# Keeping TensorE in its tiled modes between two tiled groups of matmuls: a bridge of 128x32 column tiles

## The chip, the cores and the metric

The kernel runs on one core of one Trainium2 chip. The metric is the device time of one execution in microseconds (us). Single executions of one kernel scatter by about 0.3%. "Same" means within 2%. PE is TensorE, PEld its weight loads, DVE VectorE, ACT ScalarE, POOL GpSimd, SP SyncE.

## The reference, cut to what matters

```python
def _A_ref(x, wqkv, wo):                       # linear attention, 32 heads of 16
    qkv = ...(x @ wqkv)...
    pq, pk = phi(q), phi(k)
    kv = jnp.einsum("bhsd,bhse->bhde", pk, v)
    z  = jnp.einsum("bhsd->bhd", pk)
    o  = (pq @ kv) / (pq . z)
    return o... @ wo
def _B_ref(x, w1, b1, w2, b2):                 # MLP across the 2048 tokens
    h = _layernorm(x)
    u = _gelu(jnp.einsum("bsd,sf->bdf", h, w1) + b1)      # F = 1792
    return (jnp.einsum("bdf,fs->bds", u, w2) + b2)^T
out = g * _A_ref(...) + (1 - g) * _B_ref(...)  # g = sigmoid(sum(x * gate_w))
```

x is 2048 x 512, all in bf16.

## The kernel before

The kernel never forms v. It computes G = x^T phi(k), then kv per head from wv and G, then W2 = kv Wo, so that attention ends as one matmul of normalised phi(q) with W2. kv and kv Wo need only the diagonal blocks of the heads, so both use PE as an array of small tiles. A mode is named by the rows and columns of one tile: 128x32 cuts the 128x128 array into four tiles side by side (column tiles), 32x32 into sixteen, and 128x128 is the array as a whole. A change of mode is a step from one cut to another. The stationary operand is the weights, which stay in the array; the columns of the other operand (512 in an MLP step) move through it.

```python
def kv_matmuls():                               # 64 matmuls, mode 128x32 (4 column tiles)
    kvps = bank("kvps")
    for j in range(ND):
        for k in range(ND):
            for q in range(0, P, Q32):
                c = slice(j * P + q, j * P + q + Q32)
                mm(kvps[q : q + Q32, j * Q32 : (j + 1) * Q32], wv_sb[:, k, c], gT[:, k, c],
                   k == 0, k == ND - 1, tile_position=(0, q))
    nc.vector.tensor_tensor(out=kvT..., in0=kvps..., in1=maskQ..., op=ALU.mult)   # kvT: what kv Wo reads

def w2_matmuls():                               # "kv Wo": 16 matmuls, mode 32x32 (16 tiles)
    w2ps.extend(bank("w2ps") for _ in range(ND))
    for j in range(ND):
        for i in range(NQ):
            r, c = i * Q32, (i ^ j) * Q32
            mm(w2ps[j][c : c + Q32, :], kvT[r : r + Q32, j, :], wo_sb[r : r + Q32, j, :],
               True, True, tile_position=(r, c))
```

Both stand among the blocks of the first MLP matmul. A block makes 128 rows of u from 16 steps (t) of 128x128x512 matmuls into one PSUM bank; a GELU on ACT empties it:

```python
for j in range(NB0, NF):                        # 11 blocks
    c, jj = divmod(j, FB)
    acc = bank("uacc")
    for t in range(NT):                         # 16 steps
        mm(acc[:], w1c[c][:, t, jj * P : (jj + 1) * P], hs[:, t, :], t == 0, t == NT - 1)
    gelu(j, acc)
    i = j - NB0
    if i == 2:
        kv_matmuls()
    elif i == 3:
        w2_matmuls()
    if 3 <= i < 3 + ND:
        w2_copies(i - 3)                        # ACT empties the banks of kv Wo
    ...                                         # normaliser of phi(q) on ACT and DVE, gate, loads
```

So PE goes 128x128, 128x32 (kv), 128x128 (16 steps), 32x32 (kv Wo), 128x128: four changes of mode.

## Time and profile before

| | before |
|---|---|
| time, median of 3 runs | 163.76 us (163.11 to 163.76) |
| span of the profiled run | 161.6 us |
| PE busy | 156.9 us, 97% |
| DVE, ACT busy | 124.8 us, 72.8 us |

The page of the kernel before, part 1 (busy time, share of the span, instructions) and part 4 (the chain of work that ended last, by engine and by line):

```profile
PE 156.9 (97%) x802; PEld 72.1 (45%) x817; DVE 124.8 (77%) x272; ACT 72.8 (45%) x112; POOL 7.3 (4%) x17
...
PE 97%; DVE 1%; issue 1%
...
PE uacc L110 30%; PE yps L110 30%; PE aps L110 9%; PE kacc L110 8%; PE qacc L110 8%; PE gacc L110 8%; PE wps L110 2%; PE pt L110 1%; DVE xT L208 0%; PE kvps L110 0%; PE w2ps L110 0%; DVE ot L494 0%; PE pt L331 0%
```

PE is the bound, and kv and kv Wo (kvps, w2ps) round to 0% of the chain. The page counts 802 matmuls beside 817 weight loads: 15 matmul records are missing from this trace. Where a record is missing, the view shows a hole of one step that was none.

The timeline of PE around kv and kv Wo, before (start, duration in us, line, operation, tile, shapes, count; neighbours of one kind are merged):

```profile
67.40 0.38 PE L110 MATMUL uacc<-hs,w1c 128*128 128x512 bf16 x1
67.70 0.66 PE L110 MATMUL kvps<-gT,wv_sb 128*32 128x32 bf16 x64
68.30 3.63 PE L110 MATMUL uacc<-hs,w1c 128*128 128x512 bf16 x15
71.86 0.43 PE L110 MATMUL w2ps<-wo_sb,kvT 32*32 32x512 bf16 x16
72.22 0.39 PE L110 MATMUL uacc<-hs,w1c 128*128 128x512 bf16 x1
```

PE looks busy without a break, because the record of a matmul (379 ns) is longer than the pitch at which matmuls follow one another (216 ns). The cost of a change of mode is to be read from starts, not from busy time. To the nanosecond, from the single records of the same trace:

```
from -> to, before                             starts (us)         apart   steady pitch
last MLP step -> first of kv (128x32)          67.396 -> 67.705    309 ns  216
last of kv -> first MLP step                   68.183 -> 68.299    116 ns  8
last MLP step -> first of kv Wo (32x32)        71.547 -> 71.856    309 ns  216
last of kv Wo -> first MLP step                71.906 -> 72.223    317 ns  about 216
that MLP step -> the next one                  72.223 -> 72.449    226 ns  216
```

From 10 us to the last matmul these are the only places in the kernel where two matmuls start further apart than 222 ns, missing records apart. Apart from its start-up, the kernel has no other hole on PE.

### The profile page before, as it was taken

What the parts mean: (1) busy time and instruction counts of PE and PEld (TensorE: products, weight loads), DVE (VectorE), ACT (ScalarE), POOL (GpSimd) and SP (SyncE); (2) the same over time, 40 slices, a digit from 0 to 9 for tenths busy, and PEclk for the clock granted to TensorE, in tenths of its full rate; (3) what the DMA queues carried; (4) which work ended last, traced back from release to release, by engine and by line L of the source; (5) the groups of instructions that cost most, each with busy time, mean ns of one, the idle gap of its engine ahead of it and who ended that gap; (6) DMA issues with size and microseconds to landing.
All of it is one profiled execution on the core that took longest, in us unless ns stands there. A gap on an engine that the chain in (4) does not pass through costs nothing.

```text
span 161.6 us, 2188 instructions
## 1 busy us (share of the span) xinstructions
PE 156.9 (97%) x802; PEld 72.1 (45%) x817; DVE 124.8 (77%) x272; ACT 72.8 (45%) x112; POOL 7.3 (4%) x17
## 2 busy tenths in 40 slices
PE   7999999999999999999999999999999999999993
PEld 3444444444444444444444444444444444444452
DVE  1799999957999999588599996669999999611112
ACT  3363386648667473324987123343333333111110
POOL 3000611200110000000000000000000000000000
PEclk9999999999999999999999999999999999999999
DMA  4999999999990006700940488601000001110001
GB/s 158 214 217 247 238 313 320 349 349 347 343 229 1 0 0 202 252 4 0 315 144 2 158 296 265 222 32 36 33 32 32 32 32 47 50 37 32 32 32 32
DMA packets 29241, 22.94 MB, mean 142 GB/s; under 512 B 7696, under 2 KB 29200, under 8 KB 29232
## 3 DMA queue, kind: packets, MB, share of 16 engines
q1 hardware_dynamic: 28256, 21.89, 45.6%
q10 hardware_dynamic: 864, 0.79, 1.5%
q0 software_dynamic: 112, 0.14, 0.8%
q8 instruction: 6, 0.10, 0.2%
q14 instruction: 3, 0.02, 0.1%
HBM read 19.01 MB, written 2.10 MB: 131 GB/s over the span
## 4 chain that ended last, share of the span: by engine, by line
PE 97%; DVE 1%; issue 1%
PE uacc L110 30%; PE yps L110 30%; PE aps L110 9%; PE kacc L110 8%; PE qacc L110 8%; PE gacc L110 8%; PE wps L110 2%; PE pt L110 1%; DVE xT L208 0%; PE kvps L110 0%; PE w2ps L110 0%; DVE ot L494 0%; PE pt L331 0%
## 5 line engine op out<-in xcount | busy, mean ns | idle before, releaser
L110 PE MATMUL uacc<-hs,w1c 128*128 128x512 bf16 x220 | 51.3, 379 | 0.2
L110 PE MATMUL yps<-uT,w2c 128*128 128x512 bf16 (+2 forms) x233 | 50.6, 366 | 0.3
L110 PEld LDWEIGHTS <-w2c 128*128 128x128 bf16 x238 | 22.8, 98 | 25.9
L110 PEld LDWEIGHTS <-w1c 128*128 128x128 bf16 x224 | 21.7, 98 | 26.1 <-issue 0.2
L481 ACT ACTIVATE a_sc<-aps,c,gg 128x512 f32<-128x512 f32 x16 | 12.4, 775 | 34.1 <-PE aps L110 30.5
L494 DVE SCALAR_TENSOR_TENSOR ot<-yps,c,a_sc 128x512 bf16<-128x512 f32 (+2 forms) x17 | 12.2, 716 | 16.1 <-PE yps L110 15.1
L325 ACT ACTIVATE uT<-uacc,bcol 128x512 bf16<-128x512 f32 x14 | 9.3, 686 | 18.2 <-PE uacc L110 18.1
L110 PE MATMUL kacc<-wk_sb,xT 128*128 128x512 bf16 x63 | 16.0, 380 | 0.3 <-DVE xT L208 0.2
L110 PE MATMUL qacc<-xT,wq_sb 128*128 128x512 bf16 x61 | 16.1, 379 | 0.2
L110 PE MATMUL aps<-W2sb,pqT 128*128 128x512 bf16 x63 | 16.2, 379 | 0.1
L110 PE MATMUL gacc<-pk,xs 128*128 128x512 bf16 x63 | 15.6, 379 | 0.0
L390 DVE STREAM_TRANSPOSE zT<-pz 128x512 f32<-128x512 f32 x16 | 11.3, 705 | 4.9 <-ACT pz L389 4.9
L212 ACT ACTIVATE e<-qacc 128x512 bf16<-128x512 f32 x16 | 9.6, 597 | 9.2 <-PE qacc L110 9.2
L389 ACT ACTIVATE pz<-pqT,zcol 128x512 f32<-128x512 bf16 x16 | 11.4, 714 | 4.8 <-DVE ot L494 4.7
L252 ACT ACTIVATE hs<-xs,nmr,rstd 128x512 bf16<-128x512 bf16 x16 | 12.8, 805 | 1.8 <-DVE nmr L246 1.8
L212 ACT ACTIVATE e<-kacc 128x512 bf16<-128x512 f32 x16 | 9.3, 594 | 9.2 <-PE kacc L110 9.1
L399 DVE STREAM_TRANSPOSE rex<-rd 128x512 bf16<-128x512 bf16 x16 | 11.4, 711 | 0.6
L216 DVE SCALAR_TENSOR_TENSOR pqT<-qacc,e 128x512 bf16<-128x512 f32 x16 | 11.1, 692 | 0.6
L216 DVE SCALAR_TENSOR_TENSOR pk<-kacc,e 128x512 bf16<-128x512 f32 x16 | 11.1, 692 | 0.6
L392 DVE TENSOR_REDUCE den<-zT 128x32 f32<-128x512 f32 x16 | 11.0, 686 | 0.6
L110 PEld LDWEIGHTS <-xs 128*128 128x128 bf16 x76 | 7.4, 104 | 8.5 <-DMA xs<-in_A_x_dram 1.0
L213 DVE TENSOR_SCALAR e<-e 128x512 bf16<-128x512 bf16 x32 | 9.0, 281 | 2.8 <-ACT e L212 2.8
(59 smaller groups left out, 101.0 us busy)
## 6 DMA issues: line engine op xcount, KB each, us to landing
w2c<-in_B_w_dram SPq DMA_DIRECT2D x8, 896.0 KB, 5.8
w1c<-in_B_w_dram SPq DMA_DIRECT2D x2, 2048.0 KB, 16.0
w1c<-in_B_w_dram SPq DMA_DIRECT2D x3, 1024.0 KB, 12.4
out_dram<-ot SPq DMA_DIRECT2D x13, 128.0 KB, 1.7
xs<-in_A_x_dram SPq DMA_DIRECT2D x3, 512.0 KB, 4.9
wq_sb<-in_A_wqkv_dram SPq DMA_DIRECT2D x1, 512.0 KB, 6.1
wv_sb<-in_A_wqkv_dram SPq DMA_DIRECT2D x1, 512.0 KB, 11.7
wo_sb<-in_A_wo_dram SPq DMA_DIRECT2D x1, 512.0 KB, 10.3
```

Source lines behind the costliest of these rows:

```text
L110: nc.tensor.matmul(o, lhsT=lhsT, rhs=rhs, start=start, stop=stop, **kw)
L212: nc.scalar.activation(out=e[:], in_=acc[:], func=ACT.Exp)
L213: nc.vector.tensor_scalar(out=e[:], in0=e[:], scalar1=1.0, scalar2=PHI_EPS, op0=ALU.min, op1=ALU.add)
L216: nc.vector.scalar_tensor_tensor(out=dst, in0=acc[:], scalar=0.0, in1=e[:], op0=ALU.max, op1=ALU.add)
L252: nc.scalar.activation(out=hs[:, t, :], in_=xs[:, t, :], func=ACT.Identity, scale=rstd[:, t : t + 1], bias=nmr[:, t : t + 1],)
L325: nc.scalar.activation(out=uT[:, j, :], in_=acc[:], func=ACT.Gelu_apprx_tanh, bias=bcol[:, j : j + 1])
L389: nc.scalar.activation(out=pz[:], in_=seg, func=ACT.Copy, scale=zcol[:, j : j + 1])
L390: nc.vector.transpose(out=zT[:], in_=pz[:])
L392: nc.vector.tensor_reduce(out=den[:], in_=zT[:].rearrange("p (a d) -> p a d", d=HEAD), op=ALU.add, axis=AX.X)
L399: nc.vector.transpose(out=rex[:].rearrange("p (a d) -> p a d", d=HEAD), in_=rd[:].unsqueeze(2).to_broadcast([P, SC // HEAD, HEAD]),)
L481: nc.scalar.activation(out=a_sc[:], in_=aps[:], func=ACT.Identity, scale=gg[:, t : t + 1], bias=c2[:, t : t + 1],)
L494: nc.vector.scalar_tensor_tensor(out=ot[:, :W], in0=yps[:, :W], scalar=c1[:, t : t + 1], in1=a_sc[:, cs], op0=ALU.mult, op1=ALU.add,)
```

## The change

The intent: put part of the next MLP block between kv and kv Wo in kv's own mode. Then PE goes 128x128, 128x32 (kv and three MLP steps), 32x32 (kv Wo), 128x128: three changes in place of four. Each of the three steps becomes four matmuls, one for each 32 of its 128 stationary columns; they add into the same bank, and the other 13 steps of the block follow as 128x128. The work of PE is the same. Three steps also give DVE the time to make kvT, which kv Wo needs.

```diff
+    BRIDGE = 3
     for j in range(NB0, NF):
         c, jj = divmod(j, FB)
+        i = j - NB0
         acc = bank("uacc")
         for t in range(NT):
+            if i == 3 and t < BRIDGE:
+                for q in range(0, P, Q32):
+                    c0 = jj * P + q
+                    mm(
+                        acc[q : q + Q32, :], w1c[c][:, t, c0 : c0 + Q32], hs[:, t, :],
+                        t == 0, False, tile_position=(0, q),
+                    )
+                if t == BRIDGE - 1:
+                    w2_matmuls()
+                continue
             mm(acc[:], w1c[c][:, t, jj * P : (jj + 1) * P], hs[:, t, :], t == 0, t == NT - 1)
         gelu(j, acc)
-        i = j - NB0
         if i == 2:
             kv_matmuls()
-        elif i == 3:
-            w2_matmuls()
```

## The prediction

> **What bounds the kernel now.** PE. The page gives it 156.9 us of the 161.6 us span (97%), and the chain that ended last is 97% PE. In the stretch 60 to 73 us PE is busy throughout at clock 1.00, and the waits show none that holds it (the 0.42 us before kv Wo's weight loads, put down to VectorE, is PE's own drain). Time that PE saves there should come off the end.
>
> **What a mode change costs, from starts of single PE instructions in the trace.** 128x128x512 matmuls start every 216 ns. Into kv: 67.396 to 67.705, 309 ns, 93 ns extra. Out of kv: last 128x32 start 68.183, next MLP start 68.299, 116 ns where kv's pitch is 8 ns, and the next interval is 10 ns long: 118 ns extra. Into kv Wo: 71.547 to 71.856, 93 ns extra. Out of it: 71.906 to 72.223, 317 ns, next interval 226: 112 ns extra. Together 0.42 us. The Trainium skill, "TensorEngine Tiling (Array Packing)", Key Properties, says that changing the tiling mode drains the engine; these gaps agree.
>
> **Removed:** one exit to 128x128 (118 ns) and one entry from it (93 ns).
>
> **Added:** a change from 128x32 to 32x32 between bridge and kv Wo, also a change of mode: I count a full drain, 93 ns. Three steps of 216 ns become twelve 128x32 matmuls. Column tiles run together: kv's groups of four come every 33 ns with weight loads hidden, kv Wo's 16 matmuls start within 50 ns. The skill's "TensorE: Matmul & The Clock Gate", Measured speedup vs the span model, gives one duration plus about 4 ns per further tile. So 216 to 228 ns a step, an estimate: 0 to 35 ns more in all. Column tiling gives up fast weight load, but 213 ns of streaming should hide four 92 ns loads as kv hides its own.
>
> **Moved:** kv Wo comes 3 us earlier. kv's last matmul ends at 68.37; VectorE, idle, makes kvT from 68.46 to 68.75. The bridge's last matmul starts near 68.65, kv Wo could start near 68.95: kvT is there with 0.1 to 0.2 us of slack. The copies of kv Wo's banks stay behind the block's GELU, so ScalarE and VectorE keep their order.
>
> **Sum.** From kv's last start to the next block's first start: 4.040 us before; after, about 8 + 446 + 307 + 50 + 317 + 10 + 13 x 216 = 3.946 us. Saved: 0.09 us (0 to 0.2), all on the critical path, but under 0.1% of the time and less than the spread of before's runs (163.11 to 163.76).
>
> **Predicted time:** 163.6 us, range 162.9 to 164.1. Chances: faster by over 2% 0.01, within 2% 0.98, slower by over 2% 0.01.
>
> **Right or wrong in the profile:** in the timeline no gap between kv and bridge; bridge groups 216 to 228 ns apart; kv Wo's first start about 300 ns after the last bridge start (later: kvT binds; about 220: changing between tiled modes is free); 317 ns out of kv Wo; the next block's first matmul 0.05 to 0.2 us nearer to kv's end.
>
> **What would make it wrong.** Column tiles with 512 columns not running together: 9 x 216 ns = 1.9 us more, 1.2%. Weight loads not hidden: 0.1 us a step. A wait for kvT or for kv Wo's banks, which are now taken 3 us earlier: 0.1 to 0.5 us.

## The result, and the profile after

| | before | after |
|---|---|---|
| median | 163.56 us (163.01 to 163.94, 6 runs) | 163.44 us (163.38 to 163.57, 6 runs) |
| ratio | | 0.9998, 95% interval 0.9976 to 1.002 |
| span of the profiled run | 161.553 us | 161.470 us |

All runs of before lie within 0.6% of its fastest. A ratio is the mean time of one kernel's fast runs over that of the other's of the same rounds, so it is not quite the ratio of the medians quoted beside it. No time measured here can tell a gain of 0.1 us from none. The trace can.

The page after, parts 1 and 4:

```profile
PE 157.8 (98%) x826; PEld 72.1 (45%) x826; DVE 124.8 (77%) x272; ACT 72.7 (45%) x112; POOL 7.3 (4%) x17
...
PE 98%; DVE 0%; issue 0%
```

PE's busy time seems to rise by 0.9 us. Nearly all of that is missing records: this trace has a matmul record for each of its 826 weight loads, the one before lacked 15, and each left a hole of about 53 ns (two steps of 216 ns less a record of 379), 0.8 us in all. The weight loads rose by 9, which is the change (twelve for three).

The timeline of PE in the same place, after:

```profile
67.40 0.38 PE L110 MATMUL uacc<-hs,w1c 128*128 128x512 bf16 x1
67.71 0.66 PE L110 MATMUL kvps<-gT,wv_sb 128*32 128x32 bf16 x64
68.19 0.84 PE L110 MATMUL uacc<-hs,w1c 128*32 128x512 bf16 x12
68.96 0.43 PE L110 MATMUL w2ps<-wo_sb,kvT 32*32 32x512 bf16 x16
69.33 3.19 PE L110 MATMUL uacc<-hs,w1c 128*128 128x512 bf16 x14
```

The twelve bridge matmuls follow kv without a gap (68.186 to 68.194, 8 ns). kv Wo comes at 68.96 in place of 71.86, then the other MLP steps. To the nanosecond:

```
from -> to, after                              starts (us)         apart
last of kv -> first of the bridge              68.186 -> 68.194    8 ns
first -> last start of the bridge (12)         68.194 -> 68.655    461 ns
last of the bridge -> first of kv Wo           68.655 -> 68.964    309 ns
last of kv Wo -> first MLP step                69.014 -> 69.331    317 ns
that MLP step -> the next one                  69.331 -> 69.557    226 ns
```

How far does the gain carry? Runs cannot be laid over one another from the start of the span: over seven traces whose code is the same up to kv, kv's last matmul started anywhere from 68.09 to 68.62 us, six times the gain. So I measure from kv's last start. To the second matmul of the next block it is 4.266 us before and 4.177 us after; to the very last matmul of the kernel, 90.362 and 90.273 us. The gain is 0.089 us in both places: it is made here and none of it is lost on the way to the end.

### The profile page after: what moved, and what is told of

Read it like the earlier page. It is cut to its first block, busy times and chain, and to the rows that moved or that the text cites. A ratio compares the mean times of both kernels' runs of the same rounds, so it can differ in the third digit from the quotient of the medians.

```text
span 161.5 us, 2221 instructions
## 1 busy us (share of the span) xinstructions
PE 157.8 (98%) x826; PEld 72.1 (45%) x826; DVE 124.8 (77%) x272; ACT 72.7 (45%) x112; POOL 7.3 (4%) x17
## 4 chain that ended last, share of the span: by engine, by line
PE 98%; DVE 0%; issue 0%
PE uacc L110 30%; PE yps L110 30%; PE kacc L110 9%; PE aps L110 9%; PE qacc L110 9%; PE gacc L110 9%; PE wps L110 2%; PE pt L110 1%; PE kvps L110 0%; PE w2ps L110 0%; DVE ot L503 0%; PE pt L331 0%
## 5 line engine op out<-in xcount | busy, mean ns | idle before, releaser
L110 PE MATMUL uacc<-hs,w1c 128*128 128x512 bf16 (+1 forms) x233 | 51.5, 379 | 0.0
L110 PEld LDWEIGHTS <-w1c 128*128 128x128 bf16 (+1 forms) x233 | 21.8, 98 | 26.0 <-issue 0.2
```

What stands on the lines that cost most here:

```text
L110: nc.tensor.matmul(o, lhsT=lhsT, rhs=rhs, start=start, stop=stop, **kw)
```

## The experiments

My theory: every change of mode costs PE about 0.1 us, whichever two modes it joins, and the change removes one of four; tiled steps by themselves cost what ordinary ones do. Rivals: (1) a change between two tiled modes is free and the 309 ns before kv Wo are a wait for kvT; (2) the gain comes from the earlier place of kv Wo, not from the modes; (3) the tiled steps are themselves faster or slower; (4) only leaving the tiled modes costs. Since 0.09 us cannot be timed, the first five runs repeat the piece in dispute 11 or 44 times, in the 11 MLP blocks of the kernel before. All kernels but the one marked gave the right result.

**e1_apart and e2_joined: the orders of before and after, 44 times.** The extra 32x32 group works on Wo, which has long been there, and writes to a bank that nobody reads, so it waits for nothing.

```diff
+    def dummy32():                              # dps: one extra PSUM bank
+        for i in range(NQ):
+            r = i * Q32
+            mm(dps[r : r + Q32, :], wo_sb[r : r + Q32, 0, 0:Q32], wo_sb[r : r + Q32, 0, :],
+               True, True, tile_position=(r, r))
         for t in range(NT):
+            if t % 4 == 3:                      # e1_apart; in e2_joined: t % 4 == 2
+                dummy32()
+            if t % 4 == 1:
+                ...the step as four 128x32 column tiles, as in the change
+                continue
             mm(acc[:], ...)
```

> The order of before, repeated 44 times: in each of the 11 MLP blocks after the first three, four steps are 128x32 column tiles, then comes one 128x128 step, then a group of four extra 32x32 matmuls on wo_sb into a scratch bank, then 128x128 again. Four changes of mode each time. From the gaps of the first two traces (309 ns in, 317 plus 10 ns out, 25 ns for the start of four column tiles, 10 for four 32x32 ones): 229 + 430 = 659 ns each, 29.0 us in all, about 192.6 us. This holds for every theory; it is the base for the next run.

> The order of after, repeated 44 times: the 128x128 step between the column tiles and the 32x32 group is moved behind the group, so three changes of mode in place of four. The 32x32 group needs nothing that is made late, so a wait for kvT plays no part. Theory (every change of mode costs one drain of about 0.1 us, tiled to tiled as well): 548 ns each, 24.1 us in all, 187.7 us, 4.9 us less than the run with the step between them. Rival 1 (a change between two tiled modes is free, and the 309 ns before kv Wo in the kernel after were the wait for kvT): 455 ns each, 20.0 us in all, 183.6 us, 9 us less. Rival 2 (only leaving to 128x128 costs, so one exit is saved and no entry): about 5 us less too, but then the entry gaps in the trace are near 216 ns.

**e3_dummy and e4_tiled: only the 32x32 groups, or only the column-tiled steps.** The same diff without the tiled step, or without the group.

> Only the 44 groups of four 32x32 matmuls, no column tiles: two changes of mode each. Theory: 430 ns each (216 for the group itself), 18.9 us in all, 182.5 us. If leaving and entering cost less when repeated, less.

> Only the 44 column-tiled steps, each alone between 128x128 steps: two changes of mode each, no work added. Theory: 229 ns each, 10.1 us in all, 173.7 us. Rival (column tiles cost little because weights can be loaded in the background of the other tiles): under 165 us.

**e5_adjacent: as many tiled steps, four together.** As e4_tiled with `5 <= t < 9` in place of `t % 4 == 1`.

> As many column-tiled steps as in the run with 44 lone ones, but four next to each other in each of the 11 blocks: 11 pairs of changes in place of 44. Theory (the change costs, not the tiled step): 229 ns for each of 11 groups, 2.5 us in all, 166.1 us. Rival [...]: near the run with 44 lone steps, 173.7 us.

| run | expected, theory | median | ratio to before, 95% | extra over before's median |
|---|---|---|---|---|
| e1_apart | 192.6 | 192.19 | 1.1754 (1.1737 to 1.1772) | 651 ns x 44 |
| e2_joined | 187.7 | 187.40 | 1.1454 (1.1435 to 1.1473) | 542 ns x 44 |
| e3_dummy | 182.5 | 182.32 | 1.1147 (1.113 to 1.1163) | 426 ns x 44 |
| e4_tiled | 173.7 | 173.25 | 1.0593 (1.0577 to 1.0608) | 220 ns x 44 |
| e5_adjacent | 166.1 | 165.86 | 1.0147 (1.0128 to 1.0167) | 204 ns x 11 |

The extra is the difference of the medians over the number of repeats; before had 163.56 us beside the first four and 163.62 us beside the fifth. Each miss is under 0.5 us. e1 less e2 is 109 ns for each repeat: this is the change, by time, of the size of the 89 ns in the traces of before and after, where the sequence differs a little. Rival 1 asked for about 9 us between the two; there are 4.8. e5 against e4 settles rival 3 as to cost: the same 44 tiled steps cost 9.7 us alone and 2.2 us in fours, so the pairs of changes cost, not the steps.

The weight loads of one repeat, on the timeline, first of e1_apart and then of e2_joined (in brackets the idle time of PEld before the line):

```profile
67.12 0.10 PEld L110 LDWEIGHTS <-w1c 128*32 128x32 bf16 x4 [0.42 <-issue]
67.45 0.10 PEld L110 LDWEIGHTS <-w1c 128*128 128x128 bf16 x1 [0.23 <-issue]
67.78 0.10 PEld L110 LDWEIGHTS <-wo_sb 32*32 32x32 bf16 x4 [0.23 <-issue]
68.10 0.11 PEld L110 LDWEIGHTS <-w1c 128*128 128x128 bf16 x2 [0.23 <-issue]
```

```profile
66.35 0.10 PEld L110 LDWEIGHTS <-w1c 128*32 128x32 bf16 x4 [0.42 <-issue]
66.68 0.10 PEld L110 LDWEIGHTS <-wo_sb 32*32 32x32 bf16 x4 [0.23 <-issue]
67.00 0.33 PEld L110 LDWEIGHTS <-w1c 128*128 128x128 bf16 x3 [0.23 <-issue]
67.76 0.10 PEld L110 LDWEIGHTS <-w1c 128*32 128x32 bf16 x4 [0.42 <-issue]
```

Each line but the first of each fence comes about 0.32 us after the one before it, where an undisturbed step takes 0.216 us; the last of e2_joined has two 128x128 steps ahead of it. Among 128x128 steps, weights are loaded right after the matmul before has started, a whole step ahead (in the kernel before at 66.966 us, for a matmul at 67.180). At a change of mode the load is recorded only 2 to 4 ns ahead of its own matmul (in e1_apart 67.123 for 67.125, and 67.452 for 67.456). "Issue" says that the profile sees nothing that is waited for. The record of a load (87 to 98 ns) overlaps that of its matmul, so these runs do not tell what the 0.1 us consists of: the emptying of the array, or a weight load that can no longer run ahead. They show that it comes with the change of mode.

Rival 4 falls here and in the starts: in nearly every repeat of e1 to e4 it is 309 to 310 ns into a mode (319 to 320 into 32x32 in e1_apart, where a lone step stands between two changes), 316 to 323 ns out of one, and 319 to 320 ns between the two tiled modes. The interval right after a change is about 10 ns longer than others, here as in before (226 for 216); where two changes stand one step apart this adds to the second. That is why e2_joined has 319 to 320 ns where the kernel after has 309.

**e6_bridge6: a longer bridge.** `BRIDGE = 6`.

> The kernel after with six bridge steps in place of three. kvT is then ready more than 0.6 us before kv Wo can start. Theory (drain): kv Wo's first matmul still starts 309 ns after the start of the bridge's last one, and the next block starts as far from kv's end as in the kernel after, 3.96 us. Rival (wait for kvT): the gap falls to about 216 ns and the next block comes 0.09 us earlier.

**e7_move_only: the place without the mode.** The three steps of the bridge are again `mm(acc[:], w1c[c][:, t, jj * P : (jj + 1) * P], hs[:, t, :], t == 0, False)`; kv Wo follows them as in the kernel after.

> kv Wo after three steps as in the kernel after, but the three steps are ordinary 128x128 ones: four changes of mode, only the place moved. Theory: from kv's last start to the next block's first start 4.04 us as in before, and the span is that of before, 161.55 us within 0.03. Rival (the earlier place of kv Wo gives the gain): 3.96 us and 161.47 us.

**e8_bridge_only: the mode without the place.** The bridge stays, `w2_matmuls()` goes back behind the block.

> The three tiled steps right behind kv as in the kernel after, but kv Wo stays at the end of the block, so PE leaves the tiled modes twice: four changes. Theory: 4.04 us from kv's last start to the next block's first, plus 0.02 to 0.03 us for the staggered start of the last four tiles: 4.06 us, span 161.57 us. Rival (tiled steps are themselves faster or hide the exit): below 4.0 us.

**e9_bridge1: a shorter bridge.** `BRIDGE = 1`.

> The kernel after with one bridge step in place of three. If the bridge also covers the time in which VectorE makes kvT (ready 0.57 us after kv's last start in the kernel after, visible to PE perhaps 0.06 us later, an estimate), kv Wo now waits for it: its first matmul starts about 0.63 us after kv's last start where the drain alone would allow 0.34 us, and the gain of 0.09 us turns into a loss of about 0.2 us against before. Rival (kvT is no limit): the same gain as with three or six steps.

**e10_same_mode: no change of mode before kv Wo. Wrong result.** With `BRIDGE = 6`:

```diff
-            for i in range(NQ):
-                r, c = i * Q32, (i ^ j) * Q32
-                mm(w2ps[j][c : c + Q32, :], kvT[r : r + Q32, j, :], wo_sb[r : r + Q32, j, :],
-                   True, True, tile_position=(r, c))
+            for c in range(0, P, Q32):
+                mm(w2ps[j][c : c + Q32, :], kvT[:, j, :], wo_sb[:, j, :],
+                   True, True, tile_position=(0, c))
```

> Wrong result on purpose: six bridge steps, then kv Wo as sixteen 128x32 matmuls over 512 columns in kv's own mode, with the same need for kvT. No change of mode between bridge and kv Wo. Theory (the 309 ns are the change of mode): about 191 ns from the start of the bridge's last matmul to kv Wo's first, as between any two groups of the bridge. Rival (the 309 ns belong to the step to other weights, another bank or the need for kvT): 309 ns still. kv Wo itself takes four groups of 216 ns in place of 0.27 us, so the span is longer than after's by about 0.5 us.

These five were one look each; their single times (163.28, 163.51, 163.33, 163.93, 164.2 us) are of unknown state and start at different points, so I read the traces, from kv's last start (us). Each row is one execution; e6 should equal after, and e7 before, and they do within 2 ns, which is the scatter to hold against 89 ns.

| | changes of mode | last MLP or bridge start to kv Wo | kv's last start to the second matmul of the next block | to the last matmul of the kernel |
|---|---|---|---|---|
| before | 4 | 0.309 | 4.266 | 90.362 |
| after | 3 | 0.309 | 4.177 | 90.273 |
| e6_bridge6 | 3 | 0.309 | 4.177 | 90.274 |
| e7_move_only | 4 | 0.310 | 4.268 | 90.364 |
| e8_bridge_only | 4 | 0.309 | 4.282 | 90.379 |
| e9_bridge1 | 3 | 0.586 | 4.455 | 90.551 |
| e10_same_mode | 2 | 0.191 | 4.678 | 90.774 |

- e6: the gap stays at 309 ns although kvT was ready 0.64 us earlier against kv Wo. It is no wait for kvT.
- e7: moving kv Wo alone gives nothing (2 ns). Rival 2 falls.
- e8: the bridge alone gives nothing; it loses 17 ns. The 20 to 30 ns expected for the later start of the last of four tiles are near that; nothing tests this reason. Only both together save a change. I had expected its span at 161.57 us; it was 161.48, because kv came 0.09 us earlier in this run. Measured from kv it is where the theory had it.
- e9: the sign turns. The bridge also hides the making of kvT.
- e10: with the same need for kvT and the same step to other weights and banks, but no change of mode, the gap falls from 309 to 191 ns, the same as between two groups of the bridge. So the change of mode is what costs. The kernel is still 0.5 us slower than after, since kv Wo takes four groups of 216 ns in this mode.

The timeline of PE in e6_bridge6 and then in e10_same_mode. From the first of the 24 bridge matmuls to the first of kv Wo it is 1.42 us in e6 and 1.30 us in e10, with the same steps between:

```profile
68.17 1.49 PE L110 MATMUL uacc<-hs,w1c 128*32 128x512 bf16 x24
69.59 0.43 PE L110 MATMUL w2ps<-wo_sb,kvT 32*32 32x512 bf16 x16
```

```profile
68.63 1.49 PE L110 MATMUL uacc<-hs,w1c 128*32 128x512 bf16 x24
69.93 1.05 PE L110 MATMUL w2ps<-wo_sb,kvT 128*32 128x512 bf16 x16
```

The timeline of e9_bridge1 around kv:

```profile
68.00 0.66 PE L110 MATMUL kvps<-gT,wv_sb 128*32 128x32 bf16 x64
...
68.49 0.41 PE L110 MATMUL uacc<-hs,w1c 128*32 128x512 bf16 x4
...
68.75 0.29 DVE L344 TENSOR_TENSOR kvT<-kvps,maskQ 128x128 bf16<-128x128 f32 x1 [1.45 <-PE kvps L110]
69.10 0.14 PEld L110 LDWEIGHTS <-kvT 32*32 32x32 bf16 x16 [0.50 <-DVE kvT L344]
69.10 0.44 PE L110 MATMUL w2ps<-wo_sb,kvT 32*32 32x512 bf16 x16 [0.20 <-DVE kvT L344]
```

The timeline of the kernel after has the same weight loads with a reason of the same name:

```profile
68.46 0.29 DVE L344 TENSOR_TENSOR kvT<-kvps,maskQ 128x128 bf16<-128x128 f32 x1 [1.45 <-PE kvps L110]
68.96 0.14 PEld L110 LDWEIGHTS <-kvT 32*32 32x32 bf16 x16 [0.42 <-DVE kvT L344]
68.96 0.43 PE L110 MATMUL w2ps<-wo_sb,kvT 32*32 32x512 bf16 x16
```

In e9 the wait is real: PE itself stood idle for 0.20 us, and kv Wo starts 0.05 us after kvT ends. In the kernel after, kvT had ended 0.21 us before, and PE shows no idle time: the "0.42 <-DVE kvT" only names the semaphore that came last. e6 shows that it bound nothing. From kv's last start, kv Wo could start at 0.620 us by kvT (e9) and at 0.778 us by the change of mode (after), so the slack is 0.16 us. A bridge of two steps would come to 0.562 us by the same sum (0.253 us, where the last matmul of the second step starts, and 309 ns) and would have to wait some 0.06 us; that was not run.

**e11_all_tiled: one change fewer still.** If a tiled step costs what an ordinary one does, the whole kernel can stay in 128x32 and kv needs no change at all:

```diff
     def mm(o, lhsT, rhs, start, stop, **kw):
-        nc.tensor.matmul(o, lhsT=lhsT, rhs=rhs, start=start, stop=stop, **kw)
+        if kw:
+            nc.tensor.matmul(o, lhsT=lhsT, rhs=rhs, start=start, stop=stop, **kw)
+            return
+        for q in range(0, P, Q32):
+            nc.tensor.matmul(o[q : q + Q32], lhsT=lhsT[:, q : q + Q32], rhs=rhs,
+                             start=start, stop=stop, tile_position=(0, q))
```

Its base is the kernel before; the one transpose of the biases became a matmul by the identity.

> Every matmul with 128 stationary columns, in the whole kernel, is issued as four 128x32 column tiles, so kv needs no change of mode and only two are left, around kv Wo. Theory (a tiled step costs a 128x128 step when its neighbours are tiled as well): no gap at kv, span 161.4 us or slightly less, 163.4 us, same as before within noise. Rival (four times the instructions[...] cost a few ns a step): 5 ns a step on some 740 steps would be 3.7 us more, 2%.

Measured: 164.05 us (163.57 to 164.28, 4 runs) beside 163.60 us; ratio 1.0018, 95% interval 0.9989 to 1.0046: same. The span of its profiled run is 162.427 us, 0.96 us more than after's. The steps are not the reason: from the first MLP matmul to the last matmul of the kernel it took 125.391 us, against 125.434 after and 125.522 before, with 3028 matmuls in place of 826. The missing entry into kv shows (kv starts 0.093 us sooner after the first MLP matmul than in the kernel after), though kv itself then takes 42 ns longer from its first start to its last (520 ns against 478), which I had not expected and do not explain. The loss lies before the MLP, in the stage that computes phi(k) and G. It started 0.33 us later than in the kernel after, which is within what other runs of the same start show (0.5 us between them), and met two waits of PE that the kernel after does not have, 0.13 us near 11 us and 0.53 us near 33 us, by starts. The second, on its timeline (0.36 us there, since a record is longer than a step):

```profile
30.24 0.58 ACT L219 ACTIVATE e<-kacc 128x512 bf16<-128x512 f32 x1
...
32.41 0.69 DVE L223 SCALAR_TENSOR_TENSOR pk<-kacc,e 128x512 bf16<-128x512 f32 x1
...
33.15 1.05 PE L114 MATMUL gacc<-pk,xs 128*32 128x512 bf16 x16 [0.36 <-DVE pk L223]
```

The last phi(k) tile came from ACT and DVE 1.3 to 1.5 us later than after, and G waited. The same two on the timeline of the kernel after:

```profile
28.96 0.58 ACT L212 ACTIVATE e<-kacc 128x512 bf16<-128x512 f32 x1
...
30.93 0.69 DVE L216 SCALAR_TENSOR_TENSOR pk<-kacc,e 128x512 bf16<-128x512 f32 x1
```

Whether the delay was an unlucky start of the loads, or the 23 DMA packets of instructions (0.38 MB) where after has 6 (0.10 MB) slow the loads down, is open. So I have no version that is shown to beat the kernel after.

## Why the prediction was right

- **Size and class.** Predicted 163.6 us (162.9 to 164.1), 98% for "within 2%", and 0.09 us saved. Measured 163.44 us, "same", and 0.089 us in the traces from kv's last start, to the end of the kernel.
- **The cost of a change of mode.** Predicted 93 ns in, 112 to 118 ns out. Repeated 44 times, a pair costs 220 ns with column tiles (e4_tiled), and 210 ns with 32x32 groups (e3_dummy: 426 ns less 216 for the group).
- **A change between tiled modes costs as much.** Predicted "about 300 ns after the last bridge start"; measured 309 ns, and 319 ns in e2_joined. e6_bridge6 and e10_same_mode show that it is the change of mode. That the time goes into a drain, as the prediction says, is not shown apart from a late weight load. This is why the change saves one in four and not two in four, in spite of the picture "PE leaves the tiled modes once in place of twice".
- **Column tiles run together, and their weight loads are hidden.** Predicted 216 to 228 ns a step. First starts of the bridge's groups are 220 and 216 ns apart, and e11_all_tiled holds that pace for 125 us.
- **kvT is just there.** Predicted 0.1 to 0.2 us of slack; 0.16 us by e9_bridge1 and the kernel after.
- **Two terms of the sum were off, and cancelled.** "446" for the bridge was 461 ns: its tiles start 7 to 9 ns apart and not 4. And the two sums of the prediction do not end alike: "4.040 us before" stops before the 10 ns that the second matmul after kv Wo comes late, "3.946 us" includes them. Measured to that same first start, after took 3.961 us. With both ends at the second matmul, the gain is 4.266 - 4.177 = 0.089 us. That the sum came within 5 ns of this is partly luck, since the two errors (10 and 15 ns) had opposite signs. And the range of 162.9 to 164.1 us tests little, since it holds the time of before as well: the starts are what tests the mechanism.

## What to carry to other kernels

Read the cost of a change of PE's tiling mode from starts of matmuls on both sides, since busy time and waits hide it, and count changes of mode, tiled to tiled included (128x32 to 32x32 is the one such step measured), not visits to the tiled modes. Here one change was worth about 0.1 us, so 2% of this kernel's time would take over thirty of them (an estimate: 3.3 us over 0.1); ordinary steps split into column tiles are a filler between them that costs next to nothing (17 ns in e8_bridge_only), and their number should be chosen to cover whatever the next group waits for. For a gain below the scatter of the times, repeat the disputed piece some forty times, and compare traces from a common event just ahead of the change rather than from the start of the span.

## What the Trainium skill lacked or had wrong

- "TensorEngine Tiling (Array Packing)", Key Properties, says that changing the tiling mode drains the engine, but gives no cost and does not say that a change between two tiled modes counts in full. Here: 309 ns in place of 216 into a mode, 317 ns out of 32x32 and 311 to 323 ns out of 128x32 (e5_adjacent, e4_tiled, e1_apart) with 10 ns more on the next interval, and 309 to 320 ns from 128x32 to 32x32; 220 ns for a pair by time (e4_tiled).
- The same page, Restrictions, says that column tiling switches off fast weight load, and "TensorE: Matmul & The Clock Gate", Weight-path perf modes, has it on only for loads of 128 weights, with no cost of losing it for column tiles. No run here shows whether it is off; if it is, nothing of that shows with 512 moving columns: the four 128x32 matmuls of a step take 216 ns, as one 128x128 matmul does, for 125 us on end (e11_all_tiled).
- "TensorE: Matmul & The Clock Gate", Measured speedup vs the span model, has about 4 ns for each further tile. That holds for a tile group that follows full-size steps (3 to 4 ns in e4_tiled); right behind kv's 64 small matmuls the tiles start 8 to 9 ns apart and stay so for at least six steps (e6_bridge6). In e11_all_tiled most are 2 to 5 ns apart, some 17 to 18 ns, and the step still takes 216 ns.
- The same page, Back-to-back issue gap, gives about 131 ns for a matmul of 512 columns in a sustained stream, and calls 216 ns, by the formula that it gives for isolated matmuls, too high. Here the sustained pitch is 216 ns, as that formula has it: away from the changes of mode, the starts of 128x128x512 matmuls in before and after are 215 to 216 ns apart.
